# Sums of a finished token pair ahead of the low part of h, and elementwise work moved from VectorE to GpSimd and ScalarE

## The chip, the core and the metric

One core of a Trainium2 chip runs the whole program. The engines are named as in the profile: PE is TensorE (PEld its weight loads), DVE is VectorE, ACT is ScalarE, POOL is GpSimd, and SP issues the transfers. The metric is the device time of one execution in microseconds, as the median of several runs.

## The reference, cut to what matters

Three stages follow one another: windowed attention (4 batches, 8 heads, 576 positions, head size 64), a layer with a rational activation (512 to 2048 to 512), and a mixture of 8 experts (512 to 1024 to 512 each) whose gate is balanced by eight Sinkhorn rounds. There are 2304 tokens. The weights `w_in` and `w_out` of the second stage are 64-bit floats.

```
scores = where(mask, q @ k.T / 8, -1e9)             # a band of 32, plain or with stride 4
attn   = exp(scores - max);  attn /= sum(attn) + 1e-9;  x = attn @ v
h = x @ w_in
P = a0 + a1*h + a2*h^2 + a3*h^3
Q = 1 + |b0|*|h| + |b1|*h^2
x = (P / (Q + 1e-6)) @ w_out
gate: exp(logits - max), then 8 times: rows / sum, columns / sum * N/E
out = sum over e of gate[:, e] * (relu(x @ w1[e]) @ w2[e])
```

## The kernel before, in words

Each matrix factor is held as a high and a low part (a rounded copy and what the rounding left), and each product is three matmuls: high by high, high by low, low by high.

The loop `for g in range(NS1 + NS2 + LAG2)` at the end of the kernel writes out the program. Its first 96 steps (NS1) are the rational layer: a step takes 384 tokens and 128 columns of `w_in`. `rat_l1` multiplies into the bank h1ps, `rat_a` makes the polynomial's and the denominator's first terms from it, `rat_b` the reciprocal (by Ln and Exp and one correction) and the quotient, `rat_c` the quotient's two parts, and three steps later (LAG) `rat_l2` multiplies them by `w_out`. Attention for batch 0 runs ahead of the loop; batches 1 to 3 are spread over its slots by `at` and `run_slot` (a step has four slots). The attention pieces are `att_prep` (transposes of q and k, copied out of PSUM, q with the factor 1/8), `att_qk` (scores, exponentials and the `norm` of each row), `att_tr` and `att_av`. `wi_conv` and `wo_split` turn the 64-bit weights into 32-bit ones in `to_f32`: the upper word, read as a 32-bit float, is scaled by ScalarE (L415) and shifted by VectorE (L419), VectorE joins the bits of the lower word (L420) and then the sign (L421).

The other 288 steps (NS2) are the experts: 8 experts, 9 pairs of token tiles, and 4 slices of the 1024 hidden columns each. Both layers use Strassen's scheme, so four quarter blocks take seven products. `moe_l1` multiplies one slice into a bank h2ps. `moe_a` takes it from there: ScalarE applies the relu (L804), four GpSimd sums make the combinations (L806), ScalarE writes their high part `hh` (L808) and VectorE their low part `hl` (L809). Two steps later (LAG2) `moe_l2` multiplies the parts by `w2` into four banks yps, three matmuls for each of seven products (L827 to L829); L829 is the one that reads `hl`. After the fourth slice of a pair `y_evac` empties the banks: ScalarE copies the first result (`u`, L860), seven VectorE sums combine the results (L865), and two more operations add them to the output with the gate's weight (L873). The next pair's L827 writes into the same four banks, so it waits until the sums have read them.

The raw weights of the next expert pass through two buffers (`raw_load`). VectorE scans each for its largest value (`raw_absmax`, L736); later each is loaded again and split (`raw_split`: ScalarE L141, VectorE L144, and for `w2` GpSimd differences first, L762).

The order on each engine is not written out by hand. The program is traced in the order of this code, and `TileContext(nc, schedule_with_timeline_sim=True)` then plans it: a planner steps through a simulated time and gives each engine, whenever it is free, a ready instruction, earlier ones in the traced order first. `tc.high_priority(offset=400)` in `run_slot` lets a piece count as earlier than it stands. Each engine then runs its queue in that fixed order, also where an instruction at its head has to wait. The data dependences between tiles are found by the framework; `tc.add_manual_dep` adds one more.

## Time and profile before

| | |
|---|---|
| median of 3 runs | 2131.07 us (2128.25 to 2132.69) |
| the profiled execution | 2125.07 us, its span 2123.2 us |
| PE busy | 2000.6 us (94%), 19068 matmuls |
| DVE busy | 1343.0 us (63%) |
| ACT busy | 1022.7 us (48%) |
| POOL busy | 886.2 us (42%) |
| mean granted TensorE clock | 0.973 |

A busy time is the time in which an engine ran an instruction, from the trace of one execution. Matmuls are pipelined and their ends are modelled, so a busy PE hides small gaps. The share is a mean over stages with different limits; the stages are taken apart in the rows below. A wait is the idle time of an engine just before an instruction, put down to what released it. The granted clock is a share of 2.4 GHz: 0.5 is the lower of its two levels, 1.2 GHz.

### The profile page before, as it was taken

Reading aid. Unit: us, or ns where it says so; the run is one execution under the profiler, and the core shown is the slowest. Engines: PE = TensorE matmul, PEld = TensorE weight load, DVE = VectorE, ACT = ScalarE, POOL = GpSimd, SP = SyncE. Lnnn points to the kernel's source line nnn. Section 1 sums busy time; section 2 is a strip of 40 time slices with the busy share of each in tenths; the row PEclk is TensorE's granted clock in tenths of the full one; section 3 lists DMA queues with packets and bytes.
Section 4 is the critical chain, followed back from the end, with each engine's and each line's share of the span. In section 5 each row is a group of like instructions: output and inputs, shape, how many; then the busy total and the mean of one; then the engine's idle time right before and its main releaser. Section 6 shows DMA issues by size and latency. Waiting matters only on the chain.

```text
span 2123.2 us, 46647 instructions
## 1 busy us (share of the span) xinstructions
PE 2000.6 (94%) x19068; PEld 1744.0 (82%) x19068; DVE 1343.0 (63%) x2437; ACT 1022.7 (48%) x1981; POOL 886.2 (42%) x1471
## 2 busy tenths in 40 slices
PE   6688899999999999999999999999999999999998
PEld 5466678777778898989889888988988898899997
DVE  5799989989987635555554655455465555545444
ACT  5778777867863444334333333334333333334332
POOL 1222422212354534464453446455444645535333
PEclk7789999999999999999999999999999999999999
DMA  6642311131030104001210401121040112100000
GB/s 168 183 121 79 87 25 26 25 96 51 11 100 12 41 1 120 20 23 52 69 41 1 120 6 36 51 71 41 1 120 2 41 46 75 41 2 21 31 31 31
DMA packets 171654, 112.61 MB, mean 53 GB/s; under 512 B 74160, under 2 KB 156080, under 8 KB 171440
## 3 DMA queue, kind: packets, MB, share of 16 engines
q1 hardware_dynamic: 171440, 109.64, 17.9%
q8 instruction: 149, 2.44, 0.5%
q14 instruction: 65, 0.53, 0.1%
HBM read 104.88 MB, written 4.72 MB: 52 GB/s over the span
## 4 chain that ended last, share of the span: by engine, by line
PE 49%; DVE 10%; DMA 8%; POOL 5%; ACT 3%; issue 2%; SPq 1%; DVEq 0%; POOLq 0%; ACTq 0%
PE h2ps L787 25%; DMA wraw<-in_moe_w_dram 8%; PE yps L827 8%; PE yps L829 8%; PE yps L828 8%; POOL w L762 3%; DVE sm L736 2%; POOL ht L806 2%; DVE hs L809 1%; DVE ys L865 1%; ACT w1t L141 1%; DVE w1t L144 1%; DVE slab_q L576 1%; ACT hs L808 1%; DVE slab_t L588 1%
## 5 line engine op out<-in xcount | busy, mean ns | idle before, releaser
L806 POOL TENSOR_TENSOR ht<-ht 128x128 f32<-128x128 f32 x1152 | 590.6, 532 | 735.1 <-ACT ht L804 713.6
L787 PE MATMUL h2ps<-x,w1t 128*128 128x256 f16 (+1 forms) x9216 | 822.7, 247 | 0.0
L787 PEld LDWEIGHTS <-w1t 128*128 128x128 f16 x9216 | 721.0, 98 | 59.7 <-issue 0.8
L809 DVE TENSOR_TENSOR hs<-ht,hs 128x896 f16<-128x896 f32 x288 | 319.1, 1108 | 491.9 <-ACT hs L808 490.7
L827 PE MATMUL yps<-w2t,hs 128*128 128x256 f16 x2016 | 549.9, 274 | 43.5 <-DVE ys L865 39.9
L808 ACT ACTIVATE hs<-ht 128x896 f16<-128x896 f32 x288 | 273.2, 949 | 581.7 <-POOL ht L806 581.7
L828 PE MATMUL yps<-w2t,hs 128*128 128x256 f16 x2016 | 550.2, 274 | 0.0
L829 PE MATMUL yps<-w2t,hs 128*128 128x256 f16 x2016 | 547.4, 274 | 0.1
L804 ACT ACTIVATE ht<-h2ps 128x512 f32<-128x512 f32 x288 | 170.0, 590 | 237.1 <-PE h2ps L787 230.3
L828 PEld LDWEIGHTS <-hs 128*128 128x128 f16 x2016 | 197.8, 98 | 61.0 <-issue 38.2
L827 PEld LDWEIGHTS <-hs 128*128 128x128 f16 x2016 | 197.8, 98 | 33.0 <-ACT hs L808 10.6
L829 PEld LDWEIGHTS <-hs 128*128 128x128 f16 x2016 | 198.1, 98 | 24.4 <-DVE hs L809 0.6
L596 POOL TENSOR_TENSOR slab_g<-slab_t,slab_g 128x384 fp32r<-128x384 f32 x96 | 107.5, 1122 | 231.2 <-ACT slab_g L595 188.4
L865 DVE TENSOR_TENSOR ys<-yps,ys 128x256 f32<-128x256 f32 x468 | 167.2, 415 | 55.8 <-ACT ys L860 50.6
L611 PE MATMUL o1ps<-slab_g,wo_hi 128*128 128x384 f32 x384 | 139.3, 363 | 2.2 <-POOL slab_g L596 2.0
L558 PE MATMUL h1ps<-x,wi 128*128 128x384 f16 x384 | 129.4, 337 | 7.1 <-ACT p L316 4.9
L612 PE MATMUL o1ps<-slab_g,wo_lo 128*128 128x384 f32 x384 | 132.2, 344 | 0.0
L560 PE MATMUL h1ps<-x,wi 128*128 128x384 f16 x384 | 129.1, 336 | 1.0 <-DVE wi L144 0.8
L559 PE MATMUL h1ps<-x,wi 128*128 128x384 f16 x384 | 128.9, 336 | 0.0
L610 PE MATMUL o1ps<-slab_g,wo_hi 128*128 128x384 f32 x384 | 102.7, 368 | 13.7 <-ACT slab_g L595 13.2
L736 DVE TENSOR_REDUCE sm<-wraw 128x1 f32<-128x1024 f32 x64 | 77.9, 1216 | 51.1 <-DMA wraw<-in_moe_w_dram 51.0
L322 POOL TENSOR_TENSOR p<-p,sx 128x288 f32<-128x288 f32 x48 | 36.6, 762 | 128.2 <-DVE sx L321 95.7
(143 smaller groups left out, 2387.4 us busy)
## 6 DMA issues: line engine op xcount, KB each, us to landing
wraw<-in_moe_w_dram SPq DMA_DIRECT2D x192, 256.0 KB
wraw<-in_moe_w_dram SPq DMA_DIRECT2D x128, 128.0 KB
wst<-in_moe_w_in_dram SPq DMA_DIRECT2D x16, 512.0 KB
wost<-in_moe_w_out_dram SPq DMA_DIRECT2D x16, 512.0 KB
vst<-in_v_dram SPq DMA_DIRECT2D x6, 768.0 KB
out_dram<-acc SPq DMA_DIRECT2D x16, 256.0 KB
qks<-in_q_dram SPq DMA_DIRECT2D x16, 144.0 KB
qks<-in_k_dram SPq DMA_DIRECT2D x16, 144.0 KB
```

What stands on the lines that cost most here:

```text
L558: mm = nc.tensor.matmul(hp, whi, xb[:, 0, kk, :], start=kk == 0, stop=False)
L611: nc.tensor.matmul(ob[dd], hi, d["gl"], start=False, stop=False)
L612: nc.tensor.matmul(ob[dd], lo, d["gh"], start=False, stop=last)
L787: nc.tensor.matmul(hp[:, o:o + x.shape[-1]], w[:, wh, half, kk, :], x[:, xh, kk, :], start=half == 0 and kk == 0 and wh == 0 and xh == 0 a ...
L804: nc.scalar.activation(E[:, 0:4, :].rearrange("p n c -> p (n c)"), hp, AF.Relu)
L806: nc.gpsimd.tensor_tensor(out=E[:, o, :], in0=E[:, x, :], in1=E[:, y, :], op=op)
L808: nc.scalar.activation(hh, E[:, 1:8, :], AF.Copy)
L809: nc.vector.tensor_tensor(out=hl, in0=E[:, 1:8, :], in1=hh, op=ALU.subtract)
L827: nc.tensor.matmul(o, hh[:, a - 1, :], w[:, m, 0, :], start=i == 0 and half == 0, stop=False)
L828: nc.tensor.matmul(o, hh[:, a - 1, :], w[:, m, 1, :], start=False, stop=False)
L829: nc.tensor.matmul(o, hl[:, a - 1, :], w[:, m, 0, :], start=False, stop=i == NP - 1 and (half == 1 or b == 3))
L865: nc.vector.tensor_tensor(out=o, in0=s0, in1=s1, op=ALU.add)
```

## The change

Five edits. In the experts, `moe_a` no longer issues the low part `hl`; it returns a function `low` that the loop calls after `moe_l2` and its `y_evac`, and the first `low` after a `y_evac` gets a dependence on the last of the seven sums. In the rational layer the denominator's product moves from one VectorE instruction (add b0, times |h|) to ScalarE and GpSimd: ScalarE now makes |h| first and b1*|h| + b0 from it, GpSimd multiplies. In `to_f32` ScalarE writes the sign of the upper word over that word, and a GpSimd product with it takes the place of VectorE's last bit operation. The half of q's copies that VectorE made goes to ScalarE. Two small products go from VectorE to GpSimd: the 1e-9 in the softmax's `norm`, and the scaled coefficients in `coefs`.

```diff
--- before.py
+++ after.py
@@ -20,7 +20,6 @@
 NEG = -1.0e9
 EXP_MASK = 0x7F800000
 ABS_MASK = 0x7FFFFFFF
-SIGN = -(1 << 31)
 TINY = 2.0**-80
 LN_SHIFT = 63
 
@@ -279,8 +278,6 @@
                     ps = bt[p0:p1, 0:HS].rearrange("m (c p) -> m c p", c=4)
                 if which:
                     nc.scalar.activation(dv, ps, AF.Copy)
-                elif p0 == D:
-                    nc.vector.tensor_scalar(out=dv, in0=ps, scalar1=QSCALE, scalar2=None, op0=ALU.mult)
                 else:
                     nc.scalar.activation(dv, ps, AF.Copy, scale=QSCALE)
 
@@ -317,7 +314,7 @@
             return norm
 
         def norm():
-            nc.vector.tensor_scalar(out=sx[:, 2, :], in0=sx[:, 1, :], scalar1=1e-9, scalar2=None, op0=ALU.add)
+            nc.gpsimd.tensor_scalar(out=sx[:, 2, :], in0=sx[:, 1, :], scalar1=1e-9, scalar2=None, op0=ALU.add)
             nc.vector.reciprocal(out=sx[:, 3, :], in_=sx[:, 2, :])
             nc.gpsimd.tensor_tensor(out=p, in0=p, in1=sx[:, 3, :].unsqueeze(2).to_broadcast([P, 3, KW]), op=ALU.mult)
 
@@ -413,12 +410,13 @@
         w = src.rearrange("p (n two) -> p n two", two=2)
         lo, hi = w[:, :, 0], w[:, :, 1]
         nc.scalar.activation(y, hi.bitcast(F32), AF.Copy, scale=float(2.0**-112))
+        nc.scalar.activation(hi.bitcast(F32), hi.bitcast(F32), AF.Sign)
         d = y.bitcast(I32)
 
         def bits():
             nc.vector.tensor_scalar(out=d, in0=d, scalar1=3, scalar2=None, op0=ALU.logical_shift_left)
             nc.vector.scalar_tensor_tensor(out=d, in0=lo, scalar=29, in1=d, op0=ALU.logical_shift_right, op1=ALU.bitwise_or)
-            nc.vector.scalar_tensor_tensor(out=dst.bitcast(I32), in0=hi, scalar=SIGN, in1=d, op0=ALU.bitwise_and, op1=ALU.bitwise_or)
+            nc.gpsimd.tensor_tensor(out=dst, in0=y, in1=hi.bitcast(F32), op=ALU.mult)
 
         return bits
 
@@ -489,7 +487,7 @@
             for c in range(c0, c1):
                 o = CF[:, hf, c, lo:5]
                 i = o if lo else kc
-                nc.vector.tensor_scalar(out=o, in0=i, scalar1=i_wi[:, c:c + 1], scalar2=i_x1[:, hf:hf + 1], op0=ALU.mult, op1=ALU.mult)
+                nc.gpsimd.tensor_scalar(out=o, in0=i, scalar1=i_wi[:, c:c + 1], scalar2=i_x1[:, hf:hf + 1], op0=ALU.mult, op1=ALU.mult)
 
     wi = [None] * 4
 
@@ -571,9 +569,9 @@
         a1, b0, a2, b1, a3 = cf(st)
         t, ab, qq = slab_t[:, st % 3, :], slab_a[:, st % 3, :], slab_q[:, st % 2, :]
         nc.scalar.activation(t, hp, AF.Identity, bias=a2, scale=a3)
-        nc.scalar.activation(qq, hp, AF.Abs, scale=b1)
         nc.scalar.activation(ab, hp, AF.Abs)
-        nc.vector.scalar_tensor_tensor(out=qq, in0=qq, scalar=b0, in1=ab, op0=ALU.add, op1=ALU.mult)
+        nc.scalar.activation(qq, ab, AF.Identity, bias=b0, scale=b1)
+        nc.gpsimd.tensor_tensor(out=qq, in0=qq, in1=ab, op=ALU.mult)
         nc.vector.tensor_tensor(out=t, in0=t, in1=hp, op=ALU.mult)
         nc.vector.scalar_tensor_tensor(out=t, in0=t, scalar=a1, in1=hp, op0=ALU.add, op1=ALU.mult)
         d.update(q=qq, t=t, r=ab)
@@ -806,8 +804,17 @@
             nc.gpsimd.tensor_tensor(out=E[:, o, :], in0=E[:, x, :], in1=E[:, y, :], op=op)
         hh, hl = hs[st % 3]
         nc.scalar.activation(hh, E[:, 1:8, :], AF.Copy)
-        nc.vector.tensor_tensor(out=hl, in0=E[:, 1:8, :], in1=hh, op=ALU.subtract)
         cur[NS1 + st] = hh, hl
+
+        def low():
+            i = nc.vector.tensor_tensor(out=hl, in0=E[:, 1:8, :], in1=hh, op=ALU.subtract)
+            if last_sum[0] is not None:
+                tc.add_manual_dep(i.ins, last_sum[0].name, mybir.DependencyInfo(mybir.DependencyClass.Sync, mybir.DependencyReason.DATA), reason="results first")
+                last_sum[0] = None
+
+        return low
+
+    last_sum = [None]
 
     yb = {}
     pend = []
@@ -862,7 +869,8 @@
             (v, p6, u), (x, p5, v), (w, p7, v), (d[1][:, EH:], p7, x),
             (d[0][:, 0:EH], p2, u), (d[0][:, EH:], p3, x), (d[1][:, 0:EH], p4, w),
         ):
-            nc.vector.tensor_tensor(out=o, in0=s0, in1=s1, op=ALU.add)
+            i = nc.vector.tensor_tensor(out=o, in0=s0, in1=s1, op=ALU.add)
+        last_sum[0] = i.ins
         for n in range(2):
             if e == 0:
                 if gate_ready[0]:
@@ -1078,7 +1086,7 @@
             rat_a(g)
         if ph2:
             moe_l1(g - NS1, 1)
-            moe_a(g - NS1)
+            low = moe_a(g - NS1)
         run_slot(4 * g + 1)
         l2 = LAG <= g < NS1 + LAG
         if l2:
@@ -1090,6 +1098,8 @@
             rat_c(g - 1)
         if g >= NS1 + LAG2:
             moe_l2(g - NS1 - LAG2)
+        if ph2:
+            low()
         run_slot(4 * g + 3)
     assert not slots
 
```

## Rows read from the trace of the kernel before

**Rows 1.** Busy us (instructions) by stage: PE, PEld, DVE, ACT, POOL; clock, DMA share, GB/s.

```profile
0.00:79.00 79.00, 51.05 (x374) 42.33 (x375) 48.19 (x149) 45.96 (x166) 11.29 (x33) 0.74 0.66 171
79.00:240.00 161.00, 133.00 (x881) 102.33 (x881) 152.00 (x332) 128.97 (x363) 53.36 (x54) 0.89 0.40 116
240.00:444.00 204.00, 199.93 (x1450) 159.75 (x1449) 183.80 (x391) 157.60 (x424) 60.35 (x65) 1.00 0.12 30
444.00:640.00 196.00, 182.76 (x1135) 138.30 (x1132) 183.97 (x318) 137.89 (x281) 65.07 (x64) 0.98 0.23 69
640.00:2123.00 1483.00, 1433.91 (x15232) 1301.30 (x15232) 775.05 (x1251) 552.29 (x751) 696.09 (x1256) 0.99 0.14 41
```

**Rows 2.** PE's waits in the whole span: us, times, longest.

```profile
PE yps L827 <- DVE ys L865: 39.9, 21, 4.2
PE o1ps L610 <- ACT slab_g L595: 13.2, 15, 3.9
```

**Rows 3.** Timeline, late sums, kind B, first and last: start, us, engine [idle before].

```profile
823.75 1.22 DVE L736 TENSOR_REDUCE sm<-wraw 128x1 f32<-128x1024 f32 x1 [1.48 <-DMA wraw<-in_moe_w_dram]
823.95 0.38 ACT L860 ACTIVATE ys<-yps 128x256 f32<-128x256 f32 x1
824.88 1.08 DVE L809 TENSOR_TENSOR hs<-ht,hs 128x896 f16<-128x896 f32 x1
825.88 1.21 DVE L736 TENSOR_REDUCE sm<-wraw 128x1 f32<-128x1024 f32 x1
827.48 0.37 PE L827 MATMUL yps<-w2t,hs 128*128 128x256 f16 x1 [4.22 <-DVE ys L865]
...
1762.59 0.37 PE L827 MATMUL yps<-w2t,hs 128*128 128x256 f16 x1 [4.01 <-DVE ys L865]
```

**Rows 4.** Timeline, late sums, kind A, first and last.

```profile
911.23 0.37 ACT L860 ACTIVATE ys<-yps 128x256 f32<-128x256 f32 x1
911.36 1.23 DVE L809 TENSOR_TENSOR hs<-ht,hs 128x896 f16<-128x896 f32 x1
912.98 0.27 PE L827 MATMUL yps<-w2t,hs 128*128 128x256 f16 x1 [2.24 <-DVE ys L865]
...
1846.50 0.27 PE L827 MATMUL yps<-w2t,hs 128*128 128x256 f16 x1 [2.37 <-DVE ys L865]
```

**Rows 5.** Busy time and clock after a wait of kind B.

```profile
1014.60:1018.00 3.40, 3.39 (x17) 2.36 (x17) 3.09 (x6) 1.48 (x3) 1.73 (x4) 0.51 0.72 202
```

**Rows 6.** Instructions by line and shape: count, busy us, mean ns, idle before.

```profile
L865 DVE TENSOR_TENSOR ys<-yps,ys 128x256 f32<-128x256 f32 x468 | 167.2, 415 | 55.8 <-ACT ys L860 50.6 <-PE yps L829 0.9
L873 DVE SCALAR_TENSOR_TENSOR acc<-ys,pwt,acc 128x512 f32<-128x512 f32 x112 | 88.9, 794 | 0.0
L596 POOL TENSOR_TENSOR slab_g<-slab_t,slab_g 128x384 fp32r<-128x384 f32 x96 | 107.5, 1122 | 231.2 <-ACT slab_g L595 188.4 <-issue 31.2 <-PE ptps L331 7.3
L573 ACT ACTIVATE slab_t<-h1ps,cf 128x384 f32<-128x384 f32 x96 | 64.1, 668 | 30.0 <-PE h1ps L560 17.8 <-POOL slab_g L596 11.7
L574 ACT ACTIVATE slab_q<-h1ps,cf 128x384 f32<-128x384 f32 x96 | 55.3, 576 | 7.3 <-DVE slab_a L587 7.3
L415 ACT ACTIVATE wost<-wost 128x512 f32<-128x512 f32 x16 | 10.8, 676 | 3.8 <-DMA wost<-in_moe_w_out_dram 2.4 <-POOL wo_lo L540 1.4
```

**Rows 7.** The chain that ended last, from 444 to 623 us, by line.

```profile
by line: DVE slab_q L576 10.6%; DVE slab_t L588 8.6%; DVE slab_a L587 8.5%; DVE slab_q L586 8.0%; DMA wraw<-in_moe_w_dram 7.5%; DVE slab_t L578 6.6%; DVE slab_t L577 6.3%; DVE sm L736 6.3%; DVE w2t L144 5.5%; issue 4.2%; DVE x L144 3.6%; PO
```

**Rows 8.** VectorE lines that the change removes: ns min/median/max, first and last start.

```profile
L576 DVE SCALAR_TENSOR_TENSOR slab_q<-slab_q,cf,slab_a x96: 587/612/1406, 79.4 to 620.9; 128x384 f32<-128x384 f32 x96
L283 DVE TENSOR_SCALAR qT<-qkps x24: 454/461/477, 5.6 to 416.3; 64x288 f32<-64x288 f32 x24
L320 DVE TENSOR_SCALAR sx<-sx x48: 139/160/1240, 10.6 to 443.8; 128x3 f32<-128x3 f32 x48
L421 DVE SCALAR_TENSOR_TENSOR wost<-wost x16: 660/682/1811, 78.7 to 262.1; 128x512 int32<-128x512 int32 x16
```

**Rows 9.** L576 alone from 444 to 640 us: VectorE busy us (instructions), clock, DMA.

```profile
444.00:640.00 196.00, 28.73 (x38) 0.98 0.23 69
```


## The prediction

> **What bounds the kernel now.** I read the stages first [rows 1]. From 640 us on (the experts, 1483 us) PE is busy for 1434 us and no other engine for more than 775: PE is the bound, and only its waits and its clock can be won. From 240 to 444 us PE is busy for 199.9 of 204 us, so little is to be had there. From 444 to 640 us VectorE is busy for 184.0 of 196 us and PE for 182.8; the chain that ended last decides between them, and nine VectorE entries of its row add up to 64% of this stretch [rows 7]. From 79 to 240 us VectorE is busy for 152 of 161 us, ScalarE for 129, PE for 133 at a clock of 0.89. Before 79 us no engine is at its limit.
>
> Then PE's waits [rows 2]: the largest is L827 waiting for the sums L865, 39.9 us in 21 waits. The timeline shows twelve large ones of two kinds, six each, recurring once per expert. In kind B (2.9 to 4.2 us each) [rows 3] the copy `u` ends at 823.95 + 0.38 = 824.33, but VectorE is in L736, then makes the low part L809 (1.08 us), then another L736, and the sums begin only behind it. In kind A (1.9 to 2.4 us) [rows 4] `u` ends at 911.60 and L809 holds VectorE until 911.36 + 1.23 = 912.59. The other nine waits are short. After most of kind B, and two of kind A, PE runs for 3.4 us at a granted clock of 0.51, the lower of its levels [rows 5]; seven such stretches lie in the experts' stage.
>
> **The change part by part.** The sum is made against the profiled execution, 2125.07 us (span 2123.2); the median of the runs shown, 2131.07, is 6.0 us above it, and I add that at the end.
>
> *Sums first (experts).* The L809 in both kinds belongs to the step whose `low` now depends on the last sum. So it leaves the place between `u` and the sums. Kind B: 6 x 1.08 = 6.5 us. The second L736 stays in front; if the planner now puts the sums ahead of that too, 2.29 us each, 13.7; if another piece fills the gap, 0. Kind A: 912.59 - 911.60 = 0.99 us, times 6 = 5.9 us; what is left of these waits is `u` being late on ScalarE, which nothing in the change touches. The nine short waits: 1.5 us of some 5.6. Clock: a stretch of 3.4 us at half rate costs 1.7 us, seven cost 11.9. The waits that remain are about 1.3 us (A) and 1.9 to 3.1 us (B), so I take both stretches behind A and three of five behind B as gone: 5 x 1.7 = 8.5 us (bounds 0 and 11.9). Sum 22.4 us, between 6 and 33.
>
> What the moved low part costs: behind it on VectorE are the next scans and splits. Ahead of it stand `u` (0.4 us), seven sums of 0.415 and two L873 of 0.794 [rows 6], then its own 1.08: 0.4 + 2.9 + 1.6 + 1.1 = 6.0 us after `u` can start. Its first reader, L829, comes two steps later, 2 x 1483/288 = 10.3 us. I cost it at nothing; the 4.3 us of cover go if scans and splits get between (a rival below).
>
> *The denominator's product (96 steps).* VectorE loses L576, 0.612 us undisturbed, 66.7 us in all at its mean of 0.695. ScalarE makes |h| as before, and b1*|h| + b0 in place of |h|*b1: 0.668 (L573 has the same operands) for 0.576 (L574), 96 x 0.09 = 9 us [rows 6]. GpSimd gets 96 products of 128x384; the nearest row is L596, the same shape, 1.122 us: 108 us.
>
> *Weight signs (32 pieces of 128x512, to 262 us).* VectorE loses L421, 32 x 0.68 = 22 us [rows 8]. ScalarE gets 32 sign operations at the price of L415, 0.676: 21.6 us. GpSimd gets 32 products, by columns 512/384 x 1.122 = 1.5 us: 48 us.
>
> *Copies of q.* 32 x 0.461 = 14.8 us [rows 8] go from VectorE to ScalarE, at much the same price; the two halves of a piece, now made side by side, come one after the other.
>
> *Small products.* 48 in `norm` and 24 in `coefs`, 0.16 us each on VectorE (L320's median): 11.5 us. No row shows so small a product on GpSimd; between 0.16 and L596's 1.12 I take 0.25, for they have at most 5 columns: 18 us. VectorE's reciprocal behind each now waits for GpSimd instead.
>
> Added up, phase one takes 115 us from VectorE and gives 45 to ScalarE and 174 to GpSimd. What that is worth goes by stage.
>
> *444 to 640 us:* only L576 counts. It takes 28.7 us here, 38 x 0.756 [rows 9], 0.144 above its undisturbed 0.612, and its longest is 1.406 [rows 8]: it is held up while GpSimd works. I let the second GpSimd product hold up each of the three remaining VectorE operations on two SBUF tensors (L586 to L588) in the same way: 3 x 0.144 x 38 = 16.4 us back. Net 12.3 us; PE, 182.8 us busy, leaves 13.2. The last 17 us of the stage are scans, so I take 10 (bounds: 13 gained; 14 lost, below).
>
> *79 to 240 us:* VectorE falls from 152 to about 110. But ScalarE gets some 24 signs (16 us), 12 copies (5.5) and 20 steps (2): 129 + 23 = 152. ScalarE takes VectorE's place at the same load, so I take 3 us (bounds: 12 gained, 10 lost).
>
> *Before 79 us and 240 to 444 us:* 0 (4 gained, 6 lost, from serial copies and the extra hop in `norm`), and 1 us.
>
> Sum: 22.4 + 10 + 3 + 0 + 1 = 36.4 us. 2125.07 - 36.4 + 6.0 = 2095 us.
>
> On the lock: the Trainium skill, SBUF — State Buffer, section "SBUF: two separate sides", says that VectorE and GpSimd share one pair of ports as an exclusive lock: when GpSimd's operation starts first, a VectorE operation with two SBUF inputs blocks for all of it. The maxima of 1.406 and 1.811 us in [rows 8] agree; what it would make of the time is the second rival.
>
> **Rivals.**
> *Half of it.* Either the stalls have other owners (the remaining L736, ScalarE's late `u`), or phase one gives nothing because PE and ScalarE stand right behind VectorE. For: both rows of L736 in kind B, ScalarE's sum above. Only the experts gain: 2131 - 22 = 2109; only phase one and kind A: 2131 - 14 - 6 - 3 = 2108.
> *Full blocking.* If VectorE's two-tensor operations are blocked for the whole of each added GpSimd product, the stage from 444 us gets 38 x 1.122 = 42.6 us against 28.7 taken away, 14 us lost, and the stage from 79 us its bound of 10: 2131 - 22 + 24 = 2133. Against it: L576's mean lies only 0.144 above its median with one product per step already there.
> *Low part late (slower).* A pair whose sums start 2.7 us late (kind B) and which has a scan (1.22) and a split (1.3) before the low part gets it at 6.0 + 2.7 + 2.5 = 11.2 us, past the 10.3 at which L829 wants it. From there on PE waits at L829 instead, 0.9 us or more. If that came in half of the 72 pairs with the clock dropped behind each, 36 x (0.9 + 1.7) = 94 us; with a third of that, 31 us, less phase one's 14: 2148. Against it: VectorE is busy for only 52% of this stage.
> *GpSimd's product too late (slower).* The step's chain grows: the product waits behind L596 on GpSimd and costs 1.12 instead of 0.61. Three steps lie between `rat_a` and `rat_l2`; if they no longer cover it, each of 96 steps is 0.5 us longer, 48 us: 2131 - 22 + 48 = 2157. PE already waits 13.2 us for ScalarE's L595 at the end of this chain [rows 2].
> *More.* VectorE is the one bound wherever it is near full, and the sums also overtake the second L736: 33 + 13 + 12 = 58: 2073.
>
> **How the numbers follow.** Forecast 0.40 (2083 to 2107 for its own bounds), half of it 0.30, full blocking 0.08, low part late 0.06, GpSimd's product late 0.06, more 0.10. The range 2072 to 2126 takes in forecast, half and more, 0.80. About 0.2% (4 us) is what a measurement of this kernel can tell from no change. Faster: 0.40 + 0.30 + 0.10 = 0.80; same: the blocking, 0.08; slower: 0.12.
>
> **What would show it.** Right: PE's wait L827 for L865 falls from 39.9 us to about 26, no L809 between `u` and the first sum, fewer stretches at the low clock behind 640 us; no wait of PE at L829 for L809; the stage to 640 us ends some 14 us earlier; VectorE busy near 172 us in what is now 444 to 640; GpSimd's product at 1.0 to 1.3 us. Wrong: waits at L829 or at L610 that grow by more than L827's shrink, VectorE's L586 to L588 well above 0.8 us, ScalarE full from 79 to 240 us, or the planner's new order putting other work in front of the sums.

## The result: slower by one per cent

The changed kernel took 2152.54 us (median of 4 runs, 2149.38 to 2155.09) against 2130.16 us for the kernel before in the same session: ratio 1.0104, 95% interval [1.0085, 1.0122]. The forecast was 2095 us, faster; the time lies outside its range. The profiled execution has a span of 2152.2 us, 29.0 us above the one of before; the medians differ by 22.4, so the two traces read below overstate the loss by some 7 us.

The same stages as in [rows 1], now of the changed kernel (busy us and instructions of PE, PEld, DVE, ACT, POOL; clock, DMA share, GB/s):

```profile
0.00:79.00 79.00, 54.00 (x360) 44.88 (x360) 42.04 (x115) 55.23 (x181) 27.04 (x56) 0.66 0.70 185
79.00:240.00 161.00, 130.49 (x855) 98.81 (x855) 117.82 (x229) 136.89 (x372) 117.02 (x126) 0.87 0.37 105
240.00:444.00 204.00, 195.15 (x1401) 155.43 (x1402) 165.62 (x317) 171.42 (x434) 116.17 (x124) 0.99 0.13 32
444.00:640.00 196.00, 183.07 (x1137) 139.64 (x1135) 170.51 (x283) 145.37 (x297) 107.29 (x98) 0.98 0.20 58
640.00:2123.00 1483.00, 1432.94 (x15038) 1295.62 (x15036) 782.18 (x1243) 555.37 (x755) 693.42 (x1252) 0.98 0.14 42
```

From 79 to 240 us VectorE went from 152.0 to 117.8 us (the forecast said about 110), and no engine is above 137 of 161 us; still PE does less there than before (130.5 for 133.0). The room was made and nobody used it.

Two marks in the timeline split the loss. The first relu of the experts begins at 630.35 us before and at 647.59 after: +17.2 us in the first phase. In that phase PE's idle time grows from 69.0 to 78.5 us; the other 7.7 us are matmuls that take longer, at a granted clock that is at its lower level for 106 us instead of 82. From there to the start of the last relu it takes 1479.2 us before and 1491.2 after: +12.0 us in the experts. Those two stretches, the kernel before and the changed one:

```profile
630.35:2109.55 1479.20, 1432.42 (x15202) 1299.79 (x15201) 774.15 (x1244) 555.39 (x758) 699.34 (x1262) 0.99 0.14 41
```

```profile
647.59:2138.80 1491.21, 1442.33 (x15213) 1305.00 (x15212) 782.74 (x1244) 557.91 (x757) 695.14 (x1261) 0.98 0.14 41
```

PE is idle for 46.8 us before and 48.9 after (length less busy time), so 2.1 of the 12.0 us are idle time; the other 9.9 are matmuls that take longer. The granted clock goes with it: the lower level holds for 31 us of this stage before and 55 after, at half rate some 12 us more. Not all of that can be put down to the change: one and the same kernel, profiled twice (e6 and h1 below), has 31 and 41 us there. In the changed kernel a stretch at the lower level follows all six pairs of kind B, three of kind A and one other late pair. The one that follows the late sums shown below:

```profile
1414.50:1421.30 6.80, 5.72 (x28) 3.93 (x28) 6.30 (x13) 2.39 (x3) 2.15 (x5) 0.50 0.75 224
```

PE's waits after (us, times, longest), to be held against [rows 2]; L834 is the old L827, L836 the old L829, L872 the sums, L810 the low part, L608 and L609 the old L610 and L611. The last line is of the kernel before:

```profile
PE yps L834 <- DVE ys L872: 41.2, 18, 4.5
PE o1ps L609 <- POOL slab_g L594: 13.3, 11, 5.5
PE o1ps L608 <- ACT slab_g L593: 13.1, 10, 2.9
...
PE yps L836 <- DVE hs L810: 4.9, 4, 2.5
```

```profile
PE o1ps L611 <- POOL slab_g L596: 2.0, 8, 0.4
```

The wait for the sums was to fall from 39.9 to about 26 us. It is 41.2, and a wait for the low part has come beside it (2.5 of its 4.9 us in the experts' first step). PE's wait for the low part of the quotient, which GpSimd makes in the rational layer (L594, the old L596), has grown from 2.0 to 13.3 us. Both kinds of late sums are still there. The timeline of the changed kernel (start, us, engine, line) at a pair of kind B, as in [rows 3]:

```profile
1411.85 1.22 DVE L734 TENSOR_REDUCE sm<-wraw 128x1 f32<-128x1024 f32 x1 [1.50 <-DMA wraw<-in_moe_w_dram]
1412.04 0.37 ACT L867 ACTIVATE ys<-yps 128x256 f32<-128x256 f32 x1
1412.99 1.08 DVE L810 TENSOR_TENSOR hs<-ht,hs 128x896 f16<-128x896 f32 x1
1413.99 1.21 DVE L734 TENSOR_REDUCE sm<-wraw 128x1 f32<-128x1024 f32 x1
1415.58 0.37 PE L834 MATMUL yps<-w2t,hs 128*128 128x256 f16 x1 [3.90 <-DVE ys L872]
```

And of kind A, as in [rows 4]:

```profile
927.87 0.37 ACT L867 ACTIVATE ys<-yps 128x256 f32<-128x256 f32 x1
928.00 1.23 DVE L810 TENSOR_TENSOR hs<-ht,hs 128x896 f16<-128x896 f32 x1
...
929.62 0.27 PE L834 MATMUL yps<-w2t,hs 128*128 128x256 f16 x1 [2.36 <-DVE ys L872]
```

L810 stands where L809 stood. When the last product of pair s ends, the low part ahead of the first sum is that of step s+1, which the loop traced one round earlier; `low` in this round makes s+2, and that is the one tied to the last sum. I counted the pairs in both traces: the last low part ahead of the first sum is s+1's in 71 of 72, before and after, and the last pair has no step s+1. The one that got the dependence had never stood there. All that changed in place is that it no longer runs between the sums, as it did before in 13 pairs.

The moved products, by line and shape (count, busy us, mean ns, idle before):

```profile
L574 POOL TENSOR_TENSOR slab_q<-slab_q,slab_a 128x384 f32<-128x384 f32 x96 | 107.9, 1126 | 93.1 <-ACT slab_q L573 90.0 <-DMA vt<-in_v_dram 1.6 <-PE h1ps L558 1.3
L573 ACT ACTIVATE slab_q<-slab_a,cf 128x384 f32<-128x384 f32 x96 | 67.8, 709 | 12.6 <-DVE slab_a L585 11.8
L419 POOL TENSOR_TENSOR wost<-wost 128x512 f32<-128x512 f32 x16 | 22.2, 1392 | 8.9 <-DMA vt<-in_v_dram 6.7 <-ACT wost L413 1.3 <-POOL sx L317 0.7
L317 POOL TENSOR_SCALAR sx<-sx 128x3 f32<-128x3 f32 x48 | 15.1, 315 | 45.1 <-ACT p L313 43.1
L490 POOL TENSOR_SCALAR cf<-cf,sm 128x1 f32<-128x1 f32 x8 | 8.5, 1066 | 0.1
```

The large ones cost what [rows 6] let one expect (1.126 us against 1.122; 1.39 against 1.5). The small ones don't: 0.3 to 1.1 us, where I had taken 0.25.

### The profile page after: what moved, and what is told of

It is laid out like the page before. It is cut to its first block, busy times and chain, and to the rows that moved or that the text cites. A ratio compares the mean times of both kernels' runs of the same rounds, so it can differ in the third digit from the quotient of the medians.

```text
span 2152.2 us, 46728 instructions
## 1 busy us (share of the span) xinstructions
PE 2018.3 (94%) x19068; PEld 1755.4 (82%) x19068; DVE 1290.6 (60%) x2205; ACT 1071.2 (50%) x2045; POOL 1068.1 (50%) x1671
## 4 chain that ended last, share of the span: by engine, by line
PE 49%; POOL 8%; DMA 7%; DVE 6%; ACT 4%; issue 2%; SPq 1%; DVEq 0%; POOLq 0%; ACTq 0%
PE h2ps L785 25%; PE yps L836 8%; PE yps L834 8%; PE yps L835 7%; DMA wraw<-in_moe_w_dram 7%; POOL w L760 4%; POOL ht L804 2%; DVE hs L810 1%; DVE sm L734 1%; DVE ys L872 1%; POOL slab_g L594 1%; ACT hs L806 1%; DVE w1t L143 1%; ACT ht L802 1%; ACT w2t L140 1%
## 5 line engine op out<-in xcount | busy, mean ns | idle before, releaser
L810 DVE TENSOR_TENSOR hs<-ht,hs 128x896 f16<-128x896 f32 x288 | 325.3, 1130 | 493.7 <-ACT hs L806 491.6
L834 PE MATMUL yps<-w2t,hs 128*128 128x256 f16 x2016 | 552.6, 275 | 43.9 <-DVE ys L872 41.2
L836 PE MATMUL yps<-w2t,hs 128*128 128x256 f16 x2016 | 548.9, 275 | 5.0 <-DVE hs L810 4.9
L806 ACT ACTIVATE hs<-ht 128x896 f16<-128x896 f32 x288 | 273.7, 951 | 555.3 <-POOL ht L804 555.3
L834 PEld LDWEIGHTS <-hs 128*128 128x128 f16 x2016 | 199.3, 99 | 34.8 <-ACT hs L806 11.4
L836 PEld LDWEIGHTS <-hs 128*128 128x128 f16 x2016 | 199.1, 99 | 32.3 <-DVE hs L810 7.6
L872 DVE TENSOR_TENSOR ys<-yps,ys 128x256 f32<-128x256 f32 x468 | 166.4, 416 | 55.3 <-ACT ys L867 50.2
L574 POOL TENSOR_TENSOR slab_q<-slab_q,slab_a 128x384 f32<-128x384 f32 x96 | 107.9, 1126 | 93.1 <-ACT slab_q L573 90.0
L609 PE MATMUL o1ps<-slab_g,wo_hi 128*128 128x384 f32 x384 | 140.5, 366 | 13.5 <-POOL slab_g L594 13.3
L594 POOL TENSOR_TENSOR slab_g<-slab_t,slab_g 128x384 fp32r<-128x384 f32 x96 | 112.1, 1171 | 65.9 <-ACT slab_g L593 45.7
L610 PE MATMUL o1ps<-slab_g,wo_lo 128*128 128x384 f32 x384 | 133.3, 347 | 0.0
L608 PE MATMUL o1ps<-slab_g,wo_hi 128*128 128x384 f32 x384 | 101.6, 367 | 13.4 <-ACT slab_g L593 13.1
```

Source lines behind the costliest of these rows:

```text
L594: nc.gpsimd.tensor_tensor(out=gl, in0=g, in1=gh.bitcast(F32), op=ALU.subtract)
L609: nc.tensor.matmul(ob[dd], hi, d["gl"], start=False, stop=False)
L610: nc.tensor.matmul(ob[dd], lo, d["gh"], start=False, stop=last)
L806: nc.scalar.activation(hh, E[:, 1:8, :], AF.Copy)
L810: i = nc.vector.tensor_tensor(out=hl, in0=E[:, 1:8, :], in1=hh, op=ALU.subtract)
L834: nc.tensor.matmul(o, hh[:, a - 1, :], w[:, m, 0, :], start=i == 0 and half == 0, stop=False)
```

## The experiments

Each ratio is to the kernel before, measured in the same session, with its 95% interval; 0.001 is 2.1 us. Two scatters come first, since many differences are small. Six kernels below (e1, e7, e9, g1, g2, g3) edit the experts alone, and their instructions ahead of the first relu of the experts stand in the same order as before; that relu begins at 630.9 to 634.4 us, in the kernel before at 630.4. Twelve profiles are of kernels that edit the first phase alone; their experts' stages take 1477.4 to 1482.6 us, before 1479.2. So 4 or 5 us in a mark of one profile is nothing. And the one kernel that was measured in two sessions (e6 and h1) has ratios that differ by 0.0018.

### The two halves of the change

**The low part alone (e1).**

```diff
-        nc.vector.tensor_tensor(out=hl, in0=E[:, 1:8, :], in1=hh, op=ALU.subtract)
+        def low():
+            i = nc.vector.tensor_tensor(out=hl, in0=E[:, 1:8, :], in1=hh, op=ALU.subtract)
+            if last_sum[0] is not None:
...
-            moe_a(g - NS1)
+            low = moe_a(g - NS1)
...
+        if ph2:
+            low()
```

> The kernel before with one edit alone: the low part of h traced behind moe_l2 and tied to the last sum. Theory 1 (the low part that stood in front of the sums belongs to the step before, which the dependence does not bind): the experts' stage keeps its waits of L827 for the sums near 40 us, total within 8 us of before, 2123 to 2139. Theory 2 (the later low part itself costs time at L829): the experts' stage grows by 12 us as in the changed kernel, 2143, with waits at L829. My prediction on record said 22 us less, 2109.

Measured: 1.0043 [1.0028, 1.0058]; experts' stage 1489.1 us, +9.9. PE's waits for yps in the whole span:

```profile
PE yps L836 <- DVE ys L874: 40.0, 19, 4.1
...
PE yps L836 <- ACT hs L808: 7.3, 3, 4.2
```

The wait put down to the sums is as before (39.9), that for the high part has grown from 3.1 to 7.3 us, and another for the low part has come with 3.7. The growth of the second is one wait of 4.16 us at a pair of kind B, where the first sum ends 0.02 us before the high part (1588.52 and 1588.54 us): it is one more late sum. The edit that was to give most of the gain costs 9 us by itself.

**Everything but the low part (e2).** The change's diff without `low` and `last_sum`.

> The changed kernel without the moved low part: the four other edits alone. Theory 1: the loss of phase one comes with these edits, the first expert step 15 to 20 us later than before, and the experts' stage as long as before within 6 us: 2145 to 2152. Theory 2: the first expert step 17 us later as well, but the experts' stage exactly as before: 2147. If every new order of the planner costs some 10 us in the experts' stage (theory 3), 2155 and more.

Measured: 1.0058 [1.0041, 1.0076]; first relu at 646.07 us (+15.7), experts' stage 1482.6. The two halves give 0.0043 + 0.0058 = 0.0101, against 0.0104 for the whole: they add, and both are losses. Their traces of the experts do not add: PE is idle there for 53.7 us in e1 and 43.5 in e2, against 46.8 before and 48.9 in the changed kernel, and e2, which leaves the low part alone, has 48 us at the lower clock.

### The low part: dependence, place, or ScalarE

**No dependence (e9).** As e1, `add_manual_dep` left out, so that only the traced place moves.

> The kernel before with the low part of h traced behind moe_l2, without the dependence on the last sum. If the dependence is what costs the 10 us of the low part alone (it moves the sums in the planner's time and with them the order on PE): as before, 2125 to 2133, waits of L827 for the sums near 40 us. If the place in the trace costs it: 2136 to 2142.

Measured: 1.0017 [1.0008, 1.0027]; experts' stage 1482.0, within the scatter. So of e1's 0.0043 some 0.0026, or 5.5 us, is the dependence. Two waits stand in e1's trace and not in e9's: 3.7 us for the low part, and in the pairs next after each of kind B 8.3 us for the sums, against 3.0. The planner's order differs too. It puts less other work of PE into the first seven products of a pair: 217 quarter products (matmuls of 128x256 of `moe_l1`; one of 128x128 counts a half) in all pairs but the first, against 266.5 in e9 and 284.5 before. I take it that the planned sums come earlier in its simulated time; that the thinner filling costs time was not shown.

**The low part tied where it really stood (e7).** The low part of the step before is traced in this round, behind the sums, and depends on the last of them.

```diff
-            low = moe_a(g - NS1)
+            lows.append(moe_a(g - NS1))
...
+        if len(lows) > 1 or lows and not ph2:
+            lows.pop(0)()
```

> The kernel before with the low part of each step traced one loop round later, so that it is the step right in front of the sums that is tied to the last sum. Theory 1: no low part between u and the first sum; the twelve large waits of L827 fall by about 1 us each and some of the 3.4 us stretches at the low clock go: 12 to 22 us less, 2109 to 2119. If L829 then waits for its low part (two steps less one of cover), the same or slower: 2131 and more, with waits of L829 for the low part.

Measured: 1.0091 [1.0076, 1.0106]; experts' stage 1502.2, +23. PE's waits there, from 634 to 2136 us:

```profile
PE yps L836 <- DVE ys L874: 32.1, 33, 2.1
PE yps L838 <- DVE hs L812: 16.1, 25, 1.8
PE yps L836 <- ACT hs L808: 9.7, 8, 2.3
```

This is the edit that I thought the change was: the last low part ahead of the first sum is now s's own in all 72 pairs. The longest wait for the sums halves, to 2.1 us. Two more rows of the same view, 1.8 and 1.3 us, are sums as well, those that write into other tiles; with them the total is 35.2 us, 4.7 less than before. The products with the low part now wait 16.1 us for it, those with the high part 9.7 (3.1 before). What is taken from one wait comes back more than fourfold in two others. The run is no clean test of the place alone, for the planner's order changes far more than in the others: 2044.5 quarter products stand in the first seven products of the pairs, where there were 284.5.

**No low part at all (g1).** `if st < 3:` ahead of L809; three steps fill the buffers, 285 leave it out.

> The low part of h is computed only for the first three steps; the 285 others find old values in the buffers (the results lack the low part), so VectorE's queue in the experts loses 285 operations of 0.8 to 1.2 us. If the low part in front of the sums keeps TensorE waiting, as the forecast had it, the wait for the sums falls from 40 to about 28 us and the experts' stage from 1479 to 1467 us or less. If the first sum's operand on ScalarE sets the time, the wait for the sums stays at 36 to 40 us and the stage within 4 us of 1479.

Measured: 0.9966 [0.9953, 0.9978]; experts' stage 1472.2, 7.0 us shorter. Its stretch, and PE's wait in it:

```profile
630.94:2103.14 1472.20, 1432.78 (x15203) 1299.59 (x15203) 470.38 (x960) 557.81 (x758) 624.42 (x1262) 0.99 0.14 42
```

```profile
PE yps L828 <- DVE ys L866: 32.8, 29, 3.3
```

VectorE has 304 us less to do in this stage (774 to 470), and the stage gains 7 us. I sorted PE's waits for the sums by pair. Before, kind B holds 21.7 us, kind A 13.0, the pair next after each of kind B 4.1. Without the low part: 14.2, 4.0 and 13.7. So kinds A and B do shrink when the low part is gone, by 9.0 and 7.5 us, more than the 5.9 and 6.5 that I had for it. But 9.6 us come back one pair later. (In the changed kernel the three are 13.3, 21.4 and 4.7 for A, B and the next: A and B are as before.)

The start of the sums, taken from the end of `u`, tells what of this is the low part's. In kind A they began 0.91 us after it and now begin 0.03 us after it: 6 x 0.88 = 5.3 us of the 9.0. In kind B they began 2.67 to 2.69 us after it and now begin 2.32 to 3.55 after it: without the low part they come no sooner. What else shrank goes with `u` itself, which starts earlier, seen from the finished pair's last matmul: in kind A 1.3 to 1.8 us after its end (before 3.5 to 3.9), in kind B from 1 us ahead of it to 2.6 after (before 2.1 to 3.4). Why it does so is not shown; the planner's order is another one here.

Kind A without a low part: the sums follow `u` at once, and the next pair's first product, at 909.66, waits for less than 0.1 us. What is left, 0.71 us, stands ahead of its seventh matmul, which starts as the fifth sum ends. `u` stands behind the high part and a relu on ScalarE:

```profile
907.46 0.93 ACT L808 ACTIVATE hs<-ht 128x896 f16<-128x896 f32 x1
...
908.30 0.57 ACT L804 ACTIVATE ht<-h2ps 128x512 f32<-128x512 f32 x1
908.78 0.37 ACT L861 ACTIVATE ys<-yps 128x256 f32<-128x256 f32 x1
909.18 2.61 DVE L866 TENSOR_TENSOR ys<-yps,ys 128x256 f32<-128x256 f32 x7 [0.31 <-ACT ys L861]
911.18 0.27 PE L828 MATMUL yps<-w2t,hs 128*128 128x256 f16 x1 [0.71 <-DVE ys L866]
```

Kind B, the worst of the six, where the low part was mere filler:

```profile
1195.88 0.38 ACT L861 ACTIVATE ys<-yps 128x256 f32<-128x256 f32 x1
1197.59 1.22 DVE L736 TENSOR_REDUCE sm<-wraw 128x1 f32<-128x1024 f32 x1 [0.82 <-DMA wraw<-in_moe_w_dram]
1198.72 2.27 DVE L866 TENSOR_TENSOR ys<-yps,ys 128x256 f32<-128x256 f32 x6
1199.19 0.27 PE L828 MATMUL yps<-w2t,hs 128*128 128x256 f16 x1 [3.30 <-DVE ys L866]
```

`u` is ready at 1196.26. The second scan is at the head of VectorE's queue and its transfer isn't there: VectorE stands idle for 0.82 us, then scans, and the sums begin 2.46 us after `u`. In all six pairs the second scan waits so, for 0.29 to 0.82 us; before, with the low part in front of it, in none. And a pair after a pair of kind B:

```profile
1027.00 0.72 POOL L762 TENSOR_TENSOR w<-wraw 128x256 f32<-128x256 f32 x1 [7.29 <-DMA wraw<-in_moe_w_dram]
...
1031.46 0.95 ACT L808 ACTIVATE hs<-ht 128x896 f16<-128x896 f32 x1 [8.72 <-POOL ht L806]
...
1032.79 0.38 ACT L861 ACTIVATE ys<-yps 128x256 f32<-128x256 f32 x1
1033.20 2.61 DVE L866 TENSOR_TENSOR ys<-yps,ys 128x256 f32<-128x256 f32 x7 [8.72 <-ACT ys L861]
1033.68 0.27 PE L828 MATMUL yps<-w2t,hs 128*128 128x256 f16 x1 [1.75 <-DVE ys L866]
```

VectorE has had nothing to do for 8.72 us, and PE waits 1.75 us all the same, for `u` is late. It stands on ScalarE behind a relu and the high part L808, L808 waits for GpSimd's sums L806, and those stand behind L762, a difference of raw weights, which waits 7.29 us at the head of GpSimd's queue for its transfer. In all six such pairs L762 waits 5.6 to 8.9 us for a transfer and `u` starts 5.8 us after L762 does; before, it waited 2.8 to 6.2 us in five of them. So here too a transfer of the next expert's weights sets the time, on another engine.

The planner also leaves less other work in the first seven products of the pairs, 63.5 quarter products against 284.5 before. That does not make these waits: in the pairs after kind B it is 0 against 9, and ahead of their first product stand 24 in both orders.

**The low part on GpSimd (g2).** `nc.gpsimd` for `nc.vector` in L809.

> The low part is computed, on GpSimd. By the forecast's theory VectorE comes to the sums earlier, so the wait for the sums falls as in the run without it, unless the products with the low part now wait for GpSimd (half busy there, and with a longer operation): then the wait for `hs` L809 grows from nothing to 20 us or more and the stage is longer than 1479 us. By the rival (ScalarE) nothing is gained and the same is lost.

Measured: 1.0203 [1.0182, 1.0223]; experts' stage 1517.5. PE's waits in the whole span:

```profile
PE yps L829 <- POOL hs L809: 40.9, 27, 3.2
PE yps L827 <- DVE ys L865: 19.8, 16, 3.4
```

The wait for the sums halves and one for the low part takes its place, twice as large as what went. GpSimd is busy for 1189 of the 1517 us.

**High and low part behind the sums (g3).** As e9, with ScalarE's L808 moved along.

> Both halves of the split of h, ScalarE's copy of the high part and VectorE's low part, are traced behind the pair's sums, without a dependence, so that ScalarE can take the first sum's operand before the high part of the next step. If the high part in front of that operand is what makes the sums late, the wait for the sums falls below 36 us; the stage shortens only if the products with the high part do not wait longer by as much (2 to 5 us in the kernel before). If only the planner's order of TensorE's products decides, the stage goes with the filler work inside the first 21 products (266 quarter products in all against 289 in the kernel before): 1479 to 1484 us.

Measured: 1.0007 [0.9996, 1.0018]; experts' stage 1477.8, wait for the sums 39.4 us. The quarter products number 266.5 as in e9 (284.5 before; the 289 of the expectation was a slip). Without a dependence the traced place hardly moves the order, so this run didn't test ScalarE; the late `u` is read in the timelines, and no run removes it.

### The first phase, part by part

**The denominator (e3).**

```diff
-        nc.scalar.activation(qq, hp, AF.Abs, scale=b1)
         nc.scalar.activation(ab, hp, AF.Abs)
-        nc.vector.scalar_tensor_tensor(out=qq, in0=qq, scalar=b0, in1=ab, op0=ALU.add, op1=ALU.mult)
+        nc.scalar.activation(qq, ab, AF.Identity, bias=b0, scale=b1)
+        nc.gpsimd.tensor_tensor(out=qq, in0=qq, in1=ab, op=ALU.mult)
```

> The kernel before with the denominator's product on GpSimd alone. If VectorE bounds 444 to 640 us, as the prediction had it, the first expert step comes 10 us earlier: 2121. If the longer chain through GpSimd takes what VectorE gives back, the first expert step comes 0 to 8 us later, with GpSimd and ScalarE named in the waits of PE's second product: 2131 to 2139.

Measured: 1.0007 [0.9995, 1.0018]. VectorE falls to 172.7 us from 444 to 640 us, and nothing is won.

**The signs (e4).**

```diff
+        nc.scalar.activation(hi.bitcast(F32), hi.bitcast(F32), AF.Sign)
-            nc.vector.scalar_tensor_tensor(out=dst.bitcast(I32), in0=hi, scalar=SIGN, in1=d, op0=ALU.bitwise_and, op1=ALU.bitwise_or)
+            nc.gpsimd.tensor_tensor(out=dst, in0=y, in1=hi.bitcast(F32), op=ALU.mult)
```

> The kernel before with the weights' signs on ScalarE and GpSimd alone. Theory 1 (GpSimd's queue, not its share, is what phase one pays for): 32 products of 1.3 to 1.4 us in front of the rows' normalisation and of L596 cost 0 to 8 us, the first expert step at 630 to 638, total 2129 to 2137. Theory 2 (VectorE was the bound to 262 us, so 22 us less of it is a gain): first expert step at 622 to 627, total 2120 to 2126.

Measured: 1.005 [1.0035, 1.0065]; first relu at 643.47 us. The delay grows from the first rational step (+2.8 us) to the 24th (+12 to 15, at some 270 us, where the last weights are converted) and then stays. This is the largest loss of the first phase.

**The signs cut in two (f1, f2).** f1 keeps ScalarE's sign and leaves the product on VectorE (`nc.vector.tensor_tensor`); f2 keeps the product on GpSimd and leaves ScalarE's sign out.

> The signs' edit (ratio 1.005 alone) cut in two: ScalarE's Sign pass is kept, the product of weight and sign goes back to VectorE. If the loss is ScalarE's (32 passes more in a stretch where it already waits for each weight block), this kernel is as slow as the whole edit, about 2140 us, and the first expert begins 12 us late. If the loss is the hop to GpSimd (a third engine in each block's chain, behind whatever is in front on GpSimd), this kernel is within 3 us of the kernel before, 2127 to 2133 us.

> The other half: GpSimd's product is kept, but it multiplies by the source's high word read as a number, so that ScalarE's Sign pass is left out (the weights then have wrong magnitudes, by up to two). If ScalarE's pass is the loss: within 3 us of the kernel before. If the hop to GpSimd is: about 2140 us, the first expert 12 us late. If each gives a part (the order that the planner writes moves with any of them), both kernels lie between, 2132 to 2138 us.

Measured: f1 1.0037 [1.0023, 1.0051], first relu at 636.94; f2 1.0002 [0.9992, 1.0012], 634.51. Most of the loss goes with ScalarE's pass; GpSimd's product costs nothing that can be measured. From 79 to 160 us, the kernel before, e4, f1 and f2:

```profile
79.00:160.00 81.00, 63.40 (x444) 48.60 (x444) 74.16 (x160) 61.44 (x187) 27.17 (x30) 0.83 0.50 146
```

```profile
79.00:160.00 81.00, 59.52 (x416) 45.02 (x416) 66.88 (x139) 64.68 (x194) 43.28 (x41) 0.85 0.44 133
```

```profile
79.00:160.00 81.00, 61.49 (x424) 48.46 (x425) 70.08 (x157) 66.93 (x202) 27.90 (x29) 0.83 0.50 144
```

```profile
79.00:160.00 81.00, 65.71 (x449) 51.30 (x450) 72.02 (x147) 60.17 (x187) 47.01 (x42) 0.83 0.51 151
```

In the two that lose, PE has done 2 to 4 us less and VectorE 4 to 7; in f2 PE has done 2 us more. ScalarE is at 65 to 67 of 81 us, not full, so the pass doesn't cost by its sum; whether it costs by its place in each block's chain or by the order planned around it is open, and f1's 0.0037 is not far above what the small moves below scatter by. Ahead of the first relu PE is idle for 69.0 us before, 78.0 in e4, 69.7 in f1 and 68.2 in f2: f1's profile shows no longer wait of PE, only matmuls that take longer (99 us at the lower clock, 82 before).

**The small products (e6), and again (h1).** `nc.gpsimd` in `norm` and `coefs`.

> The kernel before with the two small products (softmax sum, coefficients) on GpSimd alone. The changed kernel's coefficients took 0.6 to 1.07 us each on GpSimd, in one row, with PE waiting 5.5 us behind them. Theory 1: they cost 2 to 8 us also alone, all before 230 us: 2131 to 2137. Rival: alone, with GpSimd else little used, they are hidden: 2127 to 2131.

> The same kernel as e6_small, measured again on another pass over the chip with more rounds. If the gain is the kernel's own: ratio 0.995 to 0.997, the first expert at 625 to 628 us. If it was the pass of the chip: nearer to 1.000.

Measured: e6 0.9961 [0.9946, 0.9975], h1 0.9979 [0.9969, 0.999]; first relu at 626.47 and 626.94. This kernel beats both the kernel before and the changed one, with 2121.98 and 2123.34 us.

**The sum alone (g4), the coefficients alone (h2), all but the coefficients (e10).**

> Of the two small moves only the softmax sum's addition goes to GpSimd, the coefficients stay on VectorE. If the gain of 0.996 is the coefficients' (40 operations off VectorE just ahead of the rational steps), this one is at 1.000 within 0.002. If it is the sum's, or only the order that the planner writes, it is at 0.996 to 0.998.

> Only the coefficients go to GpSimd; the softmax sum stays on VectorE. The pair gave 0.9961 and the sum alone 1.0027. If the parts add, this one is at 0.9934 (2113 us against 2127). If the gain is the coefficients' and the sum does nothing by itself beside them, 0.996. If each small move shifts the planner's order and the times scatter by 0.3% either way, it lies anywhere from 0.996 to 1.004, and the gain of the pair has no single owner.

> The changed kernel without the moved low part and with the coefficients on VectorE: denominator, signs, copies and the softmax sum remain. If the row of coefficients on GpSimd makes the loss near 190 us: the sixteenth rational step 8 to 13 us earlier than with them (at about 221 instead of 232 us), the first expert step at 633 to 640, total 2131 to 2138. If GpSimd's products of the signs and the denominators make it: 2141 to 2147 as with the coefficients.

Measured: g4 1.0027 [1.0016, 1.0038], h2 1.0013 [1.0004, 1.0022], e10 1.0065 [1.0043, 1.0086]. The sum alone loses, the coefficients' 0.0013 is within the 0.0018 by which e6 and h1 differ, and the pair gains: nothing adds here. g4 moves 48 instructions of 128x3, and some 750 of PE's 19068 matmuls stand in another place of its order. The pair's gain repeats and belongs to that kernel's order; it has no single owner among the two moves. e10 also clears the coefficients. The trace of the changed kernel had accused them, for they stand in a row on GpSimd ahead of L574 and L594 while PE waits 5.47 us:

```profile
184.23 2.61 POOL L490 TENSOR_SCALAR cf<-cf,sm 128x1 f32<-128x1 f32 x2
...
188.99 0.99 POOL L574 TENSOR_TENSOR slab_q<-slab_q,slab_a 128x384 f32<-128x384 f32 x1
189.94 0.99 POOL L594 TENSOR_TENSOR slab_g<-slab_t,slab_g 128x384 fp32r<-128x384 f32 x1
190.99 0.69 PE L609 MATMUL o1ps<-slab_g,wo_hi 128*128 128x384 f32 x1 [5.47 <-POOL slab_g L594]
```

Without them the time is the same as e2's, though PE's waits for the low part of the quotient (L594) fall from 12.8 us in e2 to 3.1.

**With the copies of q (f3), and the denominator (f4).** e6 with the copies on ScalarE; the same with e3's edit.

> The softmax sum and the coefficients on GpSimd, which gave 0.996 alone, and the copies of q on ScalarE with them. If the gain of the small products comes from VectorE's queue ahead of the rational steps, taking the copies off VectorE too adds to it: 2117 to 2122 us. If ScalarE's queue is as late there as VectorE's was, the copies give the gain back: 2125 to 2132 us.

> The same with the denominator's product on GpSimd, that is the whole change without the signs and without the low part. If the parts add (the denominator alone gave 1.0007), as the one before to within 3 us, 2117 to 2124 us, and faster than the kernel before. If GpSimd, with small products and the denominator's on it at once, becomes late for the numerator's product, 2128 us or more, the first expert later than in the one before by 6 us or more.

Measured: f3 1.0005 [0.9995, 1.0015], f4 1.0038 [1.0023, 1.0053]. With the copies on ScalarE the gain of the small products is gone; the denominator, free by itself, costs 0.0033 beside them. The copies alone were not run, so their own price is not known.

## Why the prediction was wrong

**"The L809 in both kinds belongs to the step whose `low` now depends on the last sum."** This step failed, and with it the 22.4 us. It was one step off: the trace showed a low part in that place, not whose, and I didn't count steps. The low part ahead of the sums is the one of step s+1 (71 pairs of 72, the last having none), the dependence binds s+2's, and the wait for the sums stayed at 41.2 us. The count would have been possible on the trace of before.

**The price of that step held in kind A and failed in kind B.** I had 5.9 us for kind A; with the low part gone the sums come 5.3 us closer to `u` (g1). I had 6.5 us for kind B; there they come no closer (2.32 to 3.55 us after `u`, before 2.67 to 2.69). "The second L736 stays in front" was right, but it waits for its transfer, and the low part only filled that time. What I left out is that other waits move when these do: 9.6 us come back in the next pairs, where GpSimd waits for a transfer, the experts' stage gains 7.0, and a real move (e7) takes 4.7 us from the wait for the sums and adds 22.7 to two others.

**The moved low part "at nothing".** The products with the low part waited 4.9 us in the changed kernel, of which 2.5 stand in the experts' first step, where e2 waits 2.7 us without the move; in e1 they waited 3.7 us, and the dependence as a whole cost 5.5 (e1 against e9). The rival "low part late" has the place right, but its 31 us or more was not what made the loss: the stage's +12.0 is 2.1 us of idle time and 9.9 of slower matmuls. The clock term, 8.5 us of gain in the forecast, came out with the other sign in the one profile.

**444 to 640 us, -10.** VectorE came out as forecast (172 said, 170.5 measured), and the step that made time of it failed. From the 65th rational step to the first relu (474.2 to 630.4 us before, 488.9 to 647.6 after) VectorE has 11 us less to do, and the stretch is 2.5 us longer:

```profile
474.20:630.40 156.20, 148.47 (x904) 113.45 (x902) 152.55 (x263) 113.26 (x225) 54.09 (x49) 0.98 0.18 54
```

```profile
488.90:647.60 158.70, 146.01 (x881) 112.42 (x879) 141.51 (x224) 116.06 (x221) 92.48 (x81) 0.98 0.16 47
```

The chain that ended last, by line, in the changed kernel's stretch (in [rows 7] nine VectorE entries hold it):

```profile
by line: POOL slab_g L594 10.6%; issue 9.6%; POOL w L760 7.4%; DMA wraw<-in_moe_w_dram 7.2%; POOL slab_q L574 6.4%; DVE slab_q L584 6.3%; PE o1ps L609 4.2%; DVE slab_a L585 3.9%; PE o1ps L610 3.8%; DVE slab_t L586 3.6%; ACT slab_t L571 3.3%
```

GpSimd now leads, at 92 of 159 us busy. Its queue holds two operations of 128x384 per step (the denominator's product L574 and the quotient's low part L594) and also L760, the differences of the next expert's weights, whose transfers it waits for at its head. I had costed the product by its sum and forgot that queue. That it holds the stretch is read from this chain; e3 shows only that VectorE's time there was worth nothing.

**The lock.** I let GpSimd's second product hold up L586 to L588 by 0.144 us each. In e3, where nothing else moves, they rise by 0.085, 0.121 and 0.074 us, 38 steps of 0.28 = 10.6 us for the 16.4 I took: the mechanism was right and a third too dear. L577 and L578, with one input in PSUM, stay at 0.546 and 0.607 us (0.545 and 0.605 before). That is the rule that the Trainium skill, SBUF — State Buffer, section "SBUF: two separate sides", gives: only VectorE operations with two SBUF inputs, or in a two-port mode, meet GpSimd at the shared ports. The rival "full blocking" is refuted as a price: e3 is at 1.0007, not 14 us up.

**79 to 240 us, -3.** "ScalarE takes VectorE's place at the same load": ScalarE is at 136.9 us, not 152, so it never filled, and yet the step 24 of the rational layer comes 12 to 15 us late with the signs alone. Adding busy times can't see a chain that gets longer, if that is what happened; no run shows it. My lower bound for this stage was 10 us of loss; the signs alone exceeded it.

**Small products, 18 us.** L317 takes 0.315 us, the coefficients 0.6 to 1.07, where I had 0.25 (and on VectorE the coefficients took 0.26 to 0.36, where I had 0.16). It did not matter: the pair came out as the one gain.

The number 2152.5 falls between the rivals' 2148 and 2157, but neither mechanism made it: GpSimd's late product alone (e3) costs 0.0007, and PE's wait for the low part of the quotient behind it on GpSimd falls from 12.8 (e2) to 3.1 (e10) without a gain.

What stays open: how ScalarE's sign pass delays the conversion (through the queue on ScalarE, or through the order that the planner writes around it) was not separated, and the clock's 25 us more at the lower level were seen in one profile of the changed kernel only.

## What to carry to other kernels

Before a waiting instruction is blamed on the one in front of it, work out which iteration that one belongs to, and what is next in the queue: if that one waits for a transfer, the one in front is filler. Leaving an operation out altogether, at the price of its results, shows what moving it can be worth, and is the run to make first; then read in its trace whether the waits that shrank are those that the operation stood in. Where a planner writes the order, an edit of 48 tiny instructions moved the time by 0.27%, and 24 more with it moved it by 0.2 to 0.4% the other way, so parts don't add, and only combinations that were themselves measured count.

## What the runs showed that I had not expected

On GpSimd a product with one column took longer on average than one with five: in the changed kernel `coefs` needs 1.066 us for 128x1, 0.607 for 128x3 and 0.679 for 128x5; e6 has 1.036, 0.594 and 0.469. It is not the columns: the shortest of each shape took 0.338, 0.341 and 0.350 us, and others of the same shape up to 1.50, 1.14 and 1.36. What stretches them is not shown. On VectorE the means were 0.257, 0.276 and 0.358 us before.

ScalarE's instruction for b1*|h| + b0 takes 0.707 us from the SBUF copy of |h| (e3), against 0.668 for an instruction of the same kind from the bank h1ps [rows 6].
